# A linear-attention and SwiGLU kernel: other run lengths, orders and queues in the first 65 microseconds

## The chip, the cores and the metric

The kernel runs on one core of a Trainium2 chip. The core has five engines that run side by side, each with its own queue of instructions: PE (TensorE, matrix products and transposes into PSUM), DVE (VectorE), ACT (ScalarE), POOL (GpSimd) and SP (SyncE, which here only issues DMAs). Sixteen DMA engines move data between HBM and the on-chip memory. An engine takes its instructions strictly in the order written; an instruction whose input isn't there holds up all behind it.

The metric is the device time of one execution in microseconds (us), as the median of several. Four runs of the kernel before gave 319.65 us (319.33 to 320.38).

## The reference

Eight batches, eight heads, 576 positions, 64 numbers per head. Per batch and head a state `kv = kᵀ v` (64 by 64) is formed over all 576 positions, and `out = q kv`. Each head's row of `out` is divided by its root mean square and multiplied by `g_norm`. The heads are laid side by side into rows of 512, giving 4608 tokens; these are normalized again by their root mean square and multiplied by `rms_g`, and go through a gated feed-forward layer:

```python
kv = np.einsum('bhsd,bhse->bhde', k, v)
out = np.einsum('bhsd,bhde->bhse', q, kv)
x = (out / rms(out) * g_norm)                  # per head, then heads side by side: 4608 x 512
xn = x / rms(x) * rms_g
g, val = xn @ w_gate, xn @ w_val               # 512 -> 1536, both
y = (g * sigmoid(g) * val) @ w_out             # 1536 -> 512
```

Inputs and output are float32; the kernel computes its products in bf16 and sums in float32.

## The kernel before

The work goes by blocks of 512 tokens. Block n (0 to 7) is the first 512 positions of batch n; the last block, number 8, gathers the 64 positions left over from each batch. For each block the attention part gives `xnt`, the normalized rows turned so that the 512 features lie on partitions (four slices s of 128). The feed-forward part then does, for each of twelve slices j of 128 hidden units, four gate and four value matmuls of 128x512 (`Ffn.up`, L477), a silu on ACT (L482) and a product on DVE (L483); and for each of four row tiles c twelve matmuls with `w_out` (`down_products`, L519) and a copy to `o_sb` and to HBM (`down_out`). The attention of block n+1 is woven into the feed-forward part of block n, so that PE always has matmuls at hand. The order of each engine's instructions is written out by hand; no scheduler moves anything.

The start is different, since nothing is there to weave into. Block 0 is done in two halves of 256 tokens, A and Z (class `Cols`), while the first loads come in. SP's queue has, in this order: k of head pairs 0 and 1 (j = 0, 1; v goes by ACT's queue), half A of the queries (`load_q0(0)`, L585), k and v of pairs 2 and 3, half Z of the queries, the gate weights of blocks 0 and 1 (`load_w`, L178: 256 columns each, all rows), the value weights of blocks 0 and 1 (L182: by halves of the rows, 512 columns), the blocks 2 and 3, block 4 (four slices), then k and v of batch 1, `w_out`, the queries of batches 1 and 2. Each DMA has one of eight semaphores in turn, so a DMA is issued only after the one eight places before it has landed. The staging buffers are seven.

The chain of block 0: k and v are cast to bf16; PE forms the states (`state0`, L254); the queries are cast (`cast_q0`), turned by PE in eight 128x128 transposes per half (`turn_q0`, L642) and copied out of PSUM (`put_q0`, one copy for each two pairs of heads); products of state and turned queries (`columns`, L398) are squared on ACT; PE sums the squares (L419, L422); a short chain of small DVE operations gives the scale per head and row; DVE scales the rows (L458), PE turns them (`x_turn`, L262), DVE copies them to `xnt`. On the way `gam`, holding `rms_g` and `g_norm`, is turned by PE (L712) into columns; their product `rowscale` is multiplied into the rows of the gate and value weights when these are cast to bf16 (`round_w`; L191 on POOL and DVE, L189 on ACT). Wherever PE would idle early, `warm` (L619) puts matmuls of no use.

The first feed-forward matmuls of block 0 (`half_unit`, L494) work on two slices j at a time ("pairs", 0 and 1), for half A while Z is still being prepared: the gates of pair 0 in two parts of 128 tokens, those of pair 1, then the values of pair 0, the two transposes of Z's rows, and the values of pair 1. After that both pairs are done for half Z (in banks named `o_ps` for pair 0), and `Ffn.up` goes on from j = 4 with all 512 tokens, at about 25.8 us.

The load stream that began at 0.7 us keeps the DMA engines busy until about 48 us. Batch 1's queries come in two loads (L135), each of four heads; they are cast and turned by PE (`q_turn`, L833) in the middle of block 0's down products.

At the end of block 0 the queries of batch 2 are cast (`cast_q`, on ACT and DVE) and turned by four DMA transposes on SP's queue (`q_rows`, L300). On SP's queue the four stand between the output DMAs of block 0's first two row tiles and those of the last two, so that they also wait for the first two output copies on ACT. Batch 3's loads (`load_batch`) follow on SP's queue, in step 2 of block 1. PE reads batch 2's turned queries in step 4 of block 1 (L326).

## Time and profile before

| what | value |
|---|---|
| median of four runs | 319.65 us (319.33 to 320.38) |
| profiled execution: its own time | 319.34 us |
| its span, first to last instruction | 317.3 us |
| PE busy | 310.2 us, 98% |
| PE idle before 26 us | 3.24 us |
| mean granted TensorE clock | 0.999 |
| read from HBM, written | 37.75 MB, 9.44 MB |
| DMA issues of half A's queries (L585, two) | 1.63 to 3.06 us |
| PE's first matmuls of half Z's gates into `o_ps` (L494) | 22.29 us |
| the four DMA transposes of batch 2's queries (L300) | issued 56.05 to 63.21 us |

The page gives for each engine its busy time and share of the span. PE is the engine that is always busy after the start; the others have idle time, which costs nothing unless PE waits for them. Where the time between two stretches of PE's work goes is told by the chain of waits: followed back from the last instruction, it names at each step what released it. A line of the chain is: start, length, engine or DMA, tile and line. A line of the windows of busy time is: the window, its length, the busy time of PE, PEld (weight loads), DVE, ACT and POOL with the number of instructions, the granted clock, the DMA share and GB/s. A line of the timeline is: start, busy time, engine, line, operation, tiles and shapes, and in brackets the idle time before it with what ended it; the name in the brackets is inferred and can be another than the true one.

### The profile page before, as it was taken

The page shows a single profiled execution, that of the slowest core. Times are in us where ns is not written, and L with a number is a line of the kernel's source. Part 1 is how long each engine was busy: PE and PEld are TensorE (multiplying, and loading weights), DVE is VectorE, ACT ScalarE, POOL GpSimd, SP SyncE. Part 2 cuts the span into 40 slices and gives each one's busy share as a digit, 9 for nine tenths or more (in the row PEclk, how much of TensorE's full clock was granted, in tenths as well). Part 3 has the DMA queues.
Part 4 walks back from the last instruction along what each step waited for, and adds up shares of the span by engine and source line. Part 5 has one row for each costly group of instructions (what it writes and reads, how often), then busy time and mean ns, then how long its engine had stood idle before and what let it go on. Part 6 is the DMA issues. An engine that isn't in the chain of part 4 may idle for free.

```text
span 317.3 us, 6032 instructions
## 1 busy us (share of the span) xinstructions
PE 310.2 (98%) x2371; PEld 150.4 (47%) x2371; DVE 180.5 (57%) x378; ACT 175.5 (55%) x323; POOL 21.4 (7%) x46
## 2 busy tenths in 40 slices
PE   8899999999999999999999999999999999999995
PEld 3575455444444444444444444444444444444443
DVE  3776668679339913992289327941795079504310
ACT  3577457385667465746683768376845374233321
POOL 1264351100000000000000000000000000000000
PEclk9999999999999999999999999999999999999999
DMA  8999999677479166906790499839003710230014
GB/s 268 364 386 388 375 375 330 136 205 293 106 183 355 54 147 182 366 8 126 186 378 9 108 180 243 301 66 174 29 0 63 145 58 3 60 139 3 0 33 100
DMA packets 60712, 54.95 MB, mean 173 GB/s; under 512 B 36232, under 2 KB 45708, under 8 KB 60684
## 3 DMA queue, kind: packets, MB, share of 16 engines
q1 hardware_dynamic: 60304, 53.92, 57.4%
q10 hardware_dynamic: 380, 0.66, 0.6%
q8 instruction: 18, 0.29, 0.4%
q14 instruction: 10, 0.08, 0.1%
HBM read 37.75 MB, written 9.44 MB: 149 GB/s over the span
## 4 chain that ended last, share of the span: by engine, by line
PE 92%; DMA 5%; SPq 1%; POOL 1%; issue 0%; ACT 0%; DVE 0%
PE g_ps L477 29%; PE v_ps L477 28%; PE o_ps L519 27%; DMA st<-in_moe_w_val_dram 3%; DMA st<-in_q_dram 2%; PE att_ps L286 2%; PE g_ps L519 1%; PE v_ps L519 1%; PE v_ps L494 1%; DMA out_dram<-o_sb 1%; PE att_ps L326 1%; POOL wv_sb L191 1%; PE o_ps L494 1%; PE o_ps L326 0%; PE att_ps L262 0%; SPq L585 0%
## 5 line engine op out<-in xcount | busy, mean ns | idle before, releaser
L483 DVE TENSOR_TENSOR h_sb<-silu,v_ps 128x512 bf16<-128x512 bf16 x104 | 71.1, 683 | 100.2 <-ACT silu L482 68.0
L477 PE MATMUL g_ps<-xnt,wg_sb 128*128 128x512 bf16 x416 | 106.9, 379 | 0.0
L477 PE MATMUL v_ps<-xnt,wv_sb 128*128 128x512 bf16 x416 | 106.8, 379 | 0.0
L482 ACT ACTIVATE silu<-g_ps 128x512 bf16<-128x512 f32 x104 | 62.1, 597 | 70.2 <-PE g_ps L477 54.7
L519 PE MATMUL o_ps<-wo_sb,h_sb 128*128 128x512 bf16 x396 | 87.8, 379 | 0.0
L477 PEld LDWEIGHTS <-wv_sb 128*128 128x128 bf16 x416 | 40.7, 98 | 49.1
L519 PEld LDWEIGHTS <-h_sb 128*128 128x128 bf16 x420 | 40.6, 98 | 47.6 <-issue 0.4
L477 PEld LDWEIGHTS <-wg_sb 128*128 128x128 bf16 x416 | 39.6, 98 | 46.4
L104 ACT COPY o_sb<-o_ps 128x512 f32<-128x512 f32 (+1 forms) x34 | 19.7, 579 | 40.2 <-PE o_ps L519 39.5
L373 DVE TENSOR_TENSOR xna<-outa,s1y 128x512 bf16<-128x512 bf16 x28 | 17.9, 684 | 0.0
L104 ACT CAST vb<-st 128x576 bf16<-128x576 f32 x25 | 15.7, 673 | 3.3 <-DMA st<-in_v_dram 3.3
L104 ACT CAST qb<-st 128x512 bf16<-128x512 f32 (+1 forms) x30 | 16.3, 603 | 2.0 <-DMA st<-in_q_dram 1.9
L356 DVE TENSOR_REDUCE ssq<-sq 128x16 f32<-128x1024 bf16 x14 | 17.1, 1220 | 0.5
L356 DVE TENSOR_REDUCE ssq<-sqt 128x16 f32<-128x1024 bf16 x14 | 17.1, 1220 | 0.5
L104 ACT CAST kb<-st 128x576 bf16<-128x576 f32 x20 | 12.5, 673 | 0.0
L341 ACT ACTIVATE sq<-att_ps 128x512 bf16<-128x512 f32 x14 | 7.6, 594 | 4.3 <-PE att_ps L326 3.6
L619 PE MATMUL att_ps<-kv_all 128*128 128x512 bf16 (+1 forms) x23 | 8.1, 476 | 1.2 <-DVE sel L608 1.2
L355 DVE TENSOR_TENSOR sq<-sq,gsq 128x512 bf16<-128x512 bf16 x14 | 5.9, 422 | 4.9 <-ACT sq L341 4.9
L106 DVE CAST kb<-st 128x576 bf16<-128x576 f32 x12 | 6.0, 517 | 3.6 <-DMA st<-in_k_dram 3.5
L106 POOL CAST wo_sb<-st 128x512 bf16<-128x512 f32 x12 | 7.2, 632 | 7.4 <-DMA st<-in_moe_w_out_dram 7.4
L341 ACT ACTIVATE sqt<-o_ps 128x512 bf16<-128x512 f32 x14 | 7.6, 598 | 0.0
L347 ACT CAST outa<-o_ps 128x512 bf16<-128x512 f32 x14 | 7.5, 592 | 0.0
(148 smaller groups left out, 180.5 us busy)
## 6 DMA issues: line engine op xcount, KB each, us to landing
st<-in_k_dram SPq DMA_DIRECT2D x7, 1152.0 KB, 10.7
st<-in_v_dram SPq DMA_DIRECT2D x7, 1152.0 KB, 12.7
out_dram<-o_sb SPq DMA_DIRECT2D x14, 512.0 KB, 3.1
st<-in_q_dram SPq DMA_DIRECT2D x6, 1024.0 KB, 8.1
st<-in_moe_w_out_dram SPq DMA_DIRECT2D x6, 512.0 KB, 10.4
st<-in_moe_w_gate_dram SPq DMA_DIRECT2D x4, 512.0 KB, 10.3
st<-in_moe_w_val_dram SPq DMA_DIRECT2D x4, 512.0 KB, 9.6
st<-in_k_dram SPq DMA_DIRECT2D x4, 288.0 KB, 4.2
```

What stands on the lines that cost most here:

```text
L104: engine.copy(out=dst, in_=src)
L106: engine.tensor_copy(out=dst, in_=src)
L286: PE.matmul(self.kv_ps[x][to, a, :], lhsT=kb[rows, 2 * a + x, c, :], rhs=vb[rows, 2 * a + x, c, :], start=(a == 0 and c == 0), stop=(a == ...
L341: SC.activation(out=self.in_place(self.sq[i][:, 0], g), in_=bank, func=ACT.Square)
L347: SC.copy(out=self.in_place(rows, g), in_=bank)
L356: DVE.reduce_sum(out=self.ssq[:, c], in_=sq, axis=AX.X)
L373: DVE.tensor_tensor(out=self.xna[c], in0=self.outa[c], in1=self.alpha[:, c, :].to_broadcast([128, H, D]), op=OP.mult)
L477: PE.matmul(ps, lhsT=wt[:, s, j * 128 : (j + 1) * 128], rhs=x[:, s, :], start=(s == 0), stop=(s == NS - 1),)
L482: SC.activation(out=silu, in_=g_ps, func=ACT.Silu)
L483: DVE.tensor_tensor(out=self.h[:, j, :], in0=silu, in1=v_ps, op=OP.mult)
L519: PE.matmul(self.o_ps[c], lhsT=self.h[:, j, c * 128 : (c + 1) * 128], rhs=wo_sb[:, j, :], start=(j == 0), stop=(j == NF - 1),)
L619: PE.matmul(ps[:, 0:w], lhsT=warm_sb[:, 0:128], rhs=warm_sb[:, 0:w], start=True, stop=True, skip_group_check=True)
```

## The change

Five things, all before 65 us:

- Block 0's queries are laid so that a partition holds two heads and eight consecutive positions of each (before: four heads, four positions), in both halves. A contiguous run in HBM is 2 KB instead of 1 KB, a half comes in four DMAs of 32 partitions instead of two of 64. Casts, transposes and copies out of PSUM are as many and as large; a cast takes one head of the two, and a copy out of PSUM takes every fourth element instead of every second. The rows of block 0 so come in another order, and its output is written by four DMAs of 32 partitions for each two row tiles, instead of two of 64.
- The gate weights of blocks 0 and 1 are loaded by halves of the rows, 512 columns wide, as the value weights were; a run is 2 KB instead of 1 KB. POOL's order of rounding follows: rows s = 0, 1 of both blocks, then s = 2, 3 of block 0.
- The value matmuls of pairs 0 and 1 for half A are split by the rows of the weights (s = 0, 1 and s = 2, 3). PE's order is now: pair 0 front, pair 1 front, transpose of Z's first rows, pair 0 back, transpose of the second, pair 1 back. POOL rounds the value weights in the matching order.
- The two small loads of `gam` are issued by POOL, before it makes the identity matrices, instead of by ACT.
- At the end of block 0 all casts and all four transposes of batch 2's queries come first, ahead of all four output copies. On ACT, two casts now precede the copies of the turned rows, and the output copies come after them.

The diff (the parts left out are the loop over `round_w` for the values and the changed slices `hs0`, `hs1`, told above):

```diff
+        def half_units(self, ps, wt, j, lo, ss):
+            for u in range(2):
+                for s in ss:
+                    PE.matmul(
+                        ps[:, u, :], lhsT=wt[:, s, (j + u) * 128 : (j + u + 1) * 128],
+                        rhs=xnts[self.n][:, s, lo : lo + 256],
+                        start=(u == 0 and s == 0), stop=(u == 1 and s == NS - 1), skip_group_check=True,
+                    )
...
-                rows = out[r0 : r0 + 256, :].rearrange("(p c t) d -> t p c d", c=2, t=2)
-                for t in range(2):
-                    nc.sync.dma_start(out=rows[t], in_=self.o_sb[64 * t : 64 * t + 64])
+                rows = out[r0 : r0 + 256, :].rearrange("(p c t) d -> t p c d", c=2, t=4)
+                for t in range(4):
+                    nc.sync.dma_start(out=rows[t], in_=self.o_sb[32 * t : 32 * t + 32])
...
-        dst = q0[:, f].rearrange("(p g) h x -> p g h x", g=2)
-        for g in range(2):
-            src = q[0, 4 * g : 4 * g + 4, 256 * f : 256 * f + 256, :].rearrange("h (p t) d -> p h (t d)", t=4)
+        dst = q0[:, f].rearrange("(p g) h x -> p g h x", g=NS)
+        for g in range(NS):
+            src = q[0, 2 * g : 2 * g + 2, 256 * f : 256 * f + 256, :].rearrange("h (p t) d -> p h (t d)", t=8)
             queue.dma_start(out=dst[:, g], in_=src)
...
-    nc.scalar.dma_start(out=gam[0:NS, :], in_=moe_rms_g.rearrange("(s p) -> s p", p=128))
-    nc.scalar.dma_start(
+    nc.gpsimd.dma_start(out=gam[0:NS, :], in_=moe_rms_g.rearrange("(s p) -> s p", p=128))
+    nc.gpsimd.dma_start(
...
-    load_w("g", (0, 1), False)
-    load_w("v", (0, 1), True)
+    for name in ("g", "v"):
+        load_w(name, (0, 1), True)
...
-        ps = bank.bitcast(BF16).rearrange("p (j t x) -> p j t x", j=2, t=4)
-        for j in range(2):
-            for t in range(4):
-                PE.matmul(
-                    ps[:, j, t, :], lhsT=qb0[:, f, t, 2 * j : 2 * j + 2, :], rhs=identity,
-                    is_transpose=True, start=(j == 0 and t == 0), stop=(j == 1 and t == 3),
-                )
-        return ps.rearrange("p j t (x g) -> p j t x g", g=2)
+        ps = bank.bitcast(BF16).rearrange("p (t x) -> p t x", t=8)
+        for t in range(8):
+            PE.matmul(
+                ps[:, t, :], lhsT=qb0[:, f, t], rhs=identity, is_transpose=True, start=(t == 0), stop=(t == 7),
+            )
+        return ps.rearrange("p t (x g) -> p g t x", g=NS)
...
-    for s in range(NS):
-        round_w(0, "g", s, GP)
-    for s in (0, 1):
-        round_w(1, "g", s, GP)
+    for blk, s in ((0, 0), (0, 1), (1, 0), (1, 1), (0, 2), (0, 3)):
+        round_w(blk, "g", s, GP)
...
-    for u in range(2):
-        ffn.half_unit(first[1], u, wv_sb, u, 0, 256)
-    for u in range(2):
-        x_turn(Z, u, xs[u], DVE)
-    for u in range(2):
-        ffn.half_unit(second[1], u, wv_sb, 2 + u, 0, 256)
+    ffn.half_units(first[1], wv_sb, 0, 0, (0, 1))
+    ffn.half_units(second[1], wv_sb, 2, 0, (0, 1))
+    x_turn(Z, 0, xs[0], DVE)
+    ffn.half_units(first[1], wv_sb, 0, 0, (2, 3))
+    x_turn(Z, 1, xs[1], DVE)
+    ffn.half_units(second[1], wv_sb, 2, 0, (2, 3))
...
-    cast_q(2, 0, SC)
-    ffn.down_out(0)
+    for i in range(T):
+        cast_q(2, i, SC if i < 2 else DVE)
+    atts = {b: Att(b) for b in range(2, B + 1)}
+    for c in range(T):
+        atts[2].q_rows(c)
     down_part(1, 8, 12)
     f_x(0, xs[0], SC)
     f_x(1, xs[1], SC)
-    for i in (1, 2, 3):
-        cast_q(2, i, SC if i == 1 else DVE)
-    ffn.down_out(1)
-    atts = {b: Att(b) for b in range(2, B + 1)}
-    for c in range(2):
-        atts[2].q_rows(c)
     down_part(2, 8, 12)
     f_x(2, xs[2], DVE)
     f_x(3, xs[3], DVE)
     down_part(3, 8, 12)
-    for c in range(2, 4):
-        atts[2].q_rows(c)
-    ffn.down_out(2)
-    ffn.down_out(3)
+    for c in range(T):
+        ffn.down_out(c)
```

## The prediction

> **What bounds the kernel now.** I read the busy shares first, then the windows of busy time, the chain of waits, and the DMA rates by window.
>
> ```profile
> PE 310.2 (98%) x2371; PEld 150.4 (47%) x2371; DVE 180.5 (57%) x378; ACT 175.5 (55%) x323; POOL 21.4 (7%) x46
> 0.00:26.00 26.00, 22.76 (x249) 14.89 (x250) 15.12 (x49) 14.75 (x28) 9.97 (x28) 1.00 0.98 344
> 26.00:311.40 285.40, 285.33 (x2095) 133.65 (x2093) 165.08 (x329) 160.05 (x294) 11.41 (x19) 1.00 0.55 159
> ```
>
> From 26 to 311 us PE idles 0.07 us of 285.4, at full granted clock. The change leaves PE's instruction count alone, so it can only move the moment from which PE runs without a pause (idle before: 3.24 us, plus filler matmuls, L619), or bring a pause in. The chain shows what set that moment, and the one later place where PE paused:
>
> ```profile
> 9.33 8.83 DMA st<-in_moe_w_val_dram
> 18.25 1.85 POOL wv_sb L191 x4
> 20.14 0.83 PE v_ps L494 x6
> 20.97 0.45 PE att_ps L262 x8
> 21.42 0.87 PE v_ps L494 x8
> 22.29 1.75 PE o_ps L494 x16
> 42.60 0.17 PE g_ps L833 x3
> 42.76 0.06 issue
> 42.82 0.44 PE g_ps L833 x5
> ```
>
> The first value weights land at 18.16, four POOL roundings follow, and PE (L494) waits 0.6 us for the fourth. At 42.76 PE waits again, 0.06 us, for batch 1's queries; DVE had waited for their second half to land:
>
> ```profile
> 42.05 0.63 DVE L106 CAST qb<-st 128x512 bf16<-128x512 f32 x2 [0.72 <-DMA st<-in_q_dram]
> 18.25 2.74 POOL L191 TENSOR_SCALAR wv_sb<-st,rowscale 128x256 bf16<-128x256 f32 x6 [1.31 <-DMA st<-in_moe_w_val_dram]
> 14.19 2.74 POOL L191 TENSOR_SCALAR wg_sb<-st,rowscale 128x256 bf16<-128x256 f32 x6 [1.08 <-DVE Az L219]
> ```
>
> So two limits follow one another: PE's start-up order, and the load stream, whose DMA share is about 1 until 48 us. Whatever PE gains early is kept at 42.8 only as far as the stream is early too. The stream's rate depends on what it carries (windows 11 to 14 us, all of it runs of 1 KB, and 18 to 25 us, runs of 2 KB and more):
>
> ```profile
> DMA packets 1057, 1.05 MB, mean 349 GB/s; under 512 B 34, under 2 KB 1057, under 8 KB 1057
> DMA packets 1391, 2.71 MB, mean 387 GB/s; under 512 B 67, under 2 KB 67, under 8 KB 1391
> ```
>
> **Part 1, runs of 2 KB.** Batch 0's queries (1.05 MB) and gate blocks 0 and 1 (1.05 MB) go from 1 KB to 2 KB runs. 2.10 MB takes 6.01 us at 349 GB/s and 5.42 at 387: 0.59 us saved. The first quarter ran beside k and v at some 376 GB/s, where 0.52 MB gains only 0.04 instead of 0.15. Sum: 0.48 to 0.59; I take 0.54. Bounds: 0 (the bytes, not the runs, set the rate) to 0.70 (in the trace a packet of 1 KB took 49.5 ns and one of 2 KB 88; 2048 and 1024 of them over 16 engines are 6.34 and 5.63 us). I take the windows, which count what was moved, overlap of packets included.
>
> The Trainium skill speaks against this ("DMA: Bandwidth & Descriptors", Specifications: transfers reach line rate from 512 B on). By that the term would be 0 and the time 319.6; the two windows differ by 11% with the runs, so the trace decides. No number below uses this rule.
>
> SP issues eight query loads of 128 KB in place of four of 256 KB (1.43 and 1.27 us a pair). A new one has 64 runs; the nearest row is a k issue of 128 runs, 0.33 us, so 8 x 0.33 = 2.6 for 2.7; at the old 0.61 to 0.75 each it would be 5.4. Behind the first four stands a k load that waited for a landing until 4.35 anyway; behind the last four stands the gate load (8.14), which by SP's written order now waits for the eighth DMA before it, a k landing at 8.3. By then over 1 MB is in flight, 3 us of stream, so it costs 0. If that cover failed, each us late is a us lost. Four casts, eight transposes and four copies (0.43 to 0.69 us) keep their counts and sizes; the copies read every fourth element instead of every second. Before, reading every second cost DVE 0.69 for 512 elements, and a plain PSUM copy of 512 elements 0.69 too (45.50): I take 0, at worst 0.6 each.
>
> **Part 2, gate blocks by row halves.** A first half of both blocks lands where block 0 did (14.02, now about 13.55 with 0.47 of the gain by then). POOL rounds it at 2.74/6 = 0.457 each, but block 0's last row piece is now sixth, not fourth: 13.55 + 2.74 = 16.29 instead of 16.02. PE starts that unit at 16.39 (about 0.1 earlier now): cost 0 to 0.3 on PE there, taken as 0.1. Z's sums stand behind on PE; their result has about 0.4 us to spare below.
>
> **Part 3, value pairs by contraction halves.** The transposes for Z stood behind eight value matmuls that needed the fourth rounding. Now, with the landing at 17.62, POOL finishes its six roundings at 18.08, 18.54, 18.99, 19.45, 19.9 and 20.36. PE: first pair's front half 18.8 to 19.2, second's waits for 19.45, ends 19.8; transpose 0 (Z's first scaled rows come by 19.4) to 20.0; first pair's back half 20.4; transpose 1 20.65; second's back half 21.1. The next matmuls (L494, o_ps) start at 21.15 instead of 22.29: 1.1 us earlier. With an unmoved stream it would be 21.8, 0.45 earlier.
>
> **What is kept.** Between 22 and 42 us the stream's consumers have room: value block 4 is rounded by 31.77 for 33.42, and v of batch 1, which landed by 37.7, is cast by 40.80 for 41.28. But batch 1's queries land at 42.05 - 0.54 = 41.5, the casts end at 42.14, and PE, which would be at 41.7, pauses until 42.3. So of the 1.1 us, 0.54 + 0.06 remain at most; I take 0.55.
>
> **Part 4, batch 2's turns in one go.** SP's four transposes move from 56.05 (7.16 us, last landing about 64.4, right when PE wants it at 64.33) to after the casts, about 53.3, ahead of the outputs; they queue behind batch 2's k and v, so those are not delayed. Without this the earlier PE would wait here for up to 0.55 us; with it there are some 3 us of room. The outputs become eight issues of 128 KB behind the turns. On ACT the second query cast (0.63) now precedes the copies of rows, and four output copies go last: the last one ends about 0.15 later, before PE needs its bank at 57.38. PE cost 0. Batch 3's loads stand behind eight issues on SP, 0.33 to 0.6 each, instead of four: start 63.5 to 65.5 against 64.60, used after 75: 0.
>
> **Part 5, norm weights from POOL.** Both loads of the norm weights go from ACT, which then waited for v until 4.53, to POOL, ahead of the identity matrix. POOL was idle 10.92 us until 12.50, and PE wants the identity at 8.09 and the weights (L712) at 10.16. No row shows a DMA issued by POOL; ACT's two took 0.55 and 0.69. With those the weights are under way by 2 us: cost 0, nothing to gain. The upper end: the slowest issue in these rows, 4.35 us, twice, from 0.7 on, and 3.6 us to land as the first k did: 13.0, 2.8 us late. I take 0, since rows of the same two loads are nearest. "DMA: Bandwidth & Descriptors" (Anatomy of one DMA) puts a fixed 2.0 us on each DMA that POOL issues; by it they land near 5 us, and the trace of before has none to show it.
>
> **Sum.** The profiled execution took 319.34 (span 317.3); 319.34 - 0.55 = 318.8. The median of the four runs is 0.31 above the profiled one: 319.1.
>
> **Rivals.** (a) PE's whole 1.1 us is kept, since the queries land still earlier than the rate says. For it: in the trace fifteen of the sixteen DMA engines had brought the first value half by 16.84, and the last one, which seems to have served a 16 KB instruction fetch (1.12 us at 15.40), at 18.16; such a lag can be smaller. Time 319.65 - 1.1 = 318.5. (b) Longer runs do not speed the stream; then the queries still land at 42.05 and only 0.06 is left: 319.6. Against it stand the windows. (c) Slower: the norm weights issued by POOL land late, and PE's in-order queue stops at L712 with batch 0's columns behind it. PE can lose 0.55 there free, until 10.7 (it would wait at 42 anyway), and the next 0.55 eats the saving; from 11.3 us on the time is above that of before, us for us, and landing at 13.0 gives 319.65 + 1.7 = 321.4. For it: no such row exists; against it: 8 us of room. (d) The lag of the slowest DMA engine grows by another instruction fetch before the queries: 1.12 more on them, less 0.54: 319.65 + 0.55 = 320.2. For it: the trace has two such fetches by 26 us, and the runs spread over 1.05 us; against it: the fetches follow PE's instruction count, which is unchanged.
>
> **How the numbers follow.** A change under 0.3% (0.96 us) can hardly be told from none. Forecast 0.46 (318.7 to 319.4), (a) 0.24, (b) 0.13, (c) 0.08, (d) 0.09. (a), with the upper end of part 1, is faster by over 0.3% (0.24), and a fifth of the forecast's cases (0.09): 0.33. Slower: (c), 0.04 of (d) (a further fetch), and 0.04 for copies that double: 0.16. Same: the rest, 0.51. Range 318.1 (all of PE's gain and a little) to 320.3 ((d)); this leaves (c) and the far end of (a) out.
>
> **What would show it.** The DMA rate over 11 to 14 us near 385 GB/s; POOL's first value rounding near 17.6; L494 into o_ps near 21.2; a longer pause than 0.06 at the query turns near 42; the turns on SP near 53.5. I am wrong if the norm weights hold PE up at L712, if PE idles between 16 and 19, or if the queries of batch 1 land as late as before.

## The result, and the profile after

The changed kernel takes 320.3 us (median of 51 runs, 319.68 to 324.33) against 319.81 us for the kernel before on the same chip (76 runs, 318.76 to 321.01). The ratio is 1.0023, 95% interval 1.0015 to 1.0031; like the ratios below, it is not the quotient of the two medians (here 1.0015). I had forecast 319.1 us. The kernel became slightly slower, by less than 0.3% but clear of its interval, and the forecast had the wrong sign.

The windows of busy time of the kernel after (start and end in us; length; busy time and instructions of PE, PEld, DVE, ACT and POOL; granted clock; DMA share; GB/s):

```profile
0.00:26.00 26.00, 20.38 (x235) 13.41 (x236) 14.79 (x48) 13.80 (x25) 10.39 (x27) 1.00 0.93 330
26.00:312.80 286.80, 286.79 (x2110) 134.97 (x2108) 165.28 (x330) 161.14 (x296) 12.38 (x21) 1.00 0.55 160
10.50:12.00 1.50, 1.42 (x31) 0.85 (x32) 1.34 (x5) 0.95 (x3) 0.00 (x0) 1.00 0.87 305
12.00:13.50 1.50, 1.35 (x30) 0.80 (x28) 0.69 (x5) 0.89 (x4) 0.61 (x1) 1.00 0.86 283
13.50:15.00 1.50, 1.50 (x21) 1.24 (x22) 0.89 (x5) 0.65 (x2) 0.00 (x0) 1.00 0.90 276
```

From 26 us on PE idles 0.01 us, so the whole loss lies in the first 26. There the stream of loads is thin: 276 to 305 GB/s with DMA engines idle (share 0.86 to 0.90, where the full stream below has 1.06 to 1.09) in just the stretch in which I expected 385; over 11 to 14 us it is 281. The same windows of the kernel before have full engines:

```profile
10.50:12.00 1.50, 1.35 (x23) 0.67 (x21) 1.22 (x7) 0.87 (x2) 0.00 (x0) 1.00 1.08 333
12.00:13.50 1.50, 1.36 (x22) 0.99 (x22) 0.62 (x5) 0.89 (x2) 0.61 (x1) 1.00 1.06 355
13.50:15.00 1.50, 1.45 (x15) 0.82 (x13) 1.05 (x5) 0.66 (x2) 0.81 (x2) 1.00 1.09 363
```

SP's queue tells why (timeline of SP: start, us, line, DMA, count). The kernel after:

```profile
1.64 2.71 SPq L595 DMA_DIRECT2D st<-in_q_dram  x4
...
6.77 2.54 SPq L595 DMA_DIRECT2D st<-in_q_dram  x4
9.35 1.10 SPq L182 DMA_DIRECT2D st<-in_moe_w_gate_dram  x2
```

The kernel before:

```profile
1.63 1.43 SPq L585 DMA_DIRECT2D st<-in_q_dram  x2
...
6.82 1.27 SPq L585 DMA_DIRECT2D st<-in_q_dram  x2
8.14 1.15 SPq L178 DMA_DIRECT2D st<-in_moe_w_gate_dram  x2
```

A query load costs SP 0.64 to 0.72 us on average, whether it is 256 KB or 128 KB. Eight of them take 5.25 us instead of 2.70, and the gate loads go out at 9.35 instead of 8.14. The chain of waits of the kernel after carries this on to PE:

```profile
9.98 7.76 DMA st<-in_moe_w_gate_dram
17.74 0.08 issue
17.82 1.10 POOL wg_sb L191 x2
...
18.97 0.45 PE g_ps L494 x5
...
23.71 1.91 PE o_ps L494 x16
...
44.18 0.45 PE g_ps L841 x8
```

The second gate half, issued at 9.98, lands at 17.74; POOL rounds it, and PE, which could have gone on at 17.2, waits. Part of this landing is the lag of one DMA engine: by the landing records of the sixteen engines, fifteen had brought their shares by 16.45 and the last at 17.74, 1.29 us later. Without part 1 (the first experiment below) the sixteen bring this half within 14.23 to 15.13. So the late issue and the thin stream account for about 1.3 us of the landing (16.45 against 15.13), and the one engine for the rest. The waits of PE over the first 30 us have the line

```profile
PE g_ps L494 <- POOL wg_sb L191: 1.6, 2, 1.3
```

that is, 1.6 us in two waits, the longest 1.3. The matmuls of L494 into o_ps start at 23.71, against 22.29 before and 21.15 forecast. Those 1.42 us, less the 0.06 that PE no longer pauses at batch 1's query turns (44.18), are the 1.32 us between the two profiled executions (320.66 and 319.34). Over all runs the medians differ by 0.5: the profiled execution of the kernel before was 0.47 below its median and that of the kernel after 0.36 above. How thin the stream gets and how the engines finish differ from trace to trace: a later kernel with the same loads (the one with more fillers) had 202, 318 and 332 GB/s in the same three windows, and its second gate half landed at 16.55, the last engine 0.06 us behind the fifteenth.

### The profile page after: what moved, and what is told of

It is laid out like the page before. It is cut to its first block, busy times and chain, and to the rows that moved or that the text cites. A ratio compares the mean times of both kernels' runs of the same rounds, so it can differ in the third digit from the quotient of the medians.

```text
span 318.8 us, 6049 instructions
## 1 busy us (share of the span) xinstructions
PE 309.1 (97%) x2371; PEld 150.1 (47%) x2371; DVE 180.4 (57%) x378; ACT 175.6 (55%) x323; POOL 22.8 (7%) x48
## 4 chain that ended last, share of the span: by engine, by line
PE 92%; DMA 5%; SPq 1%; POOL 0%; DVE 0%; issue 0%; ACT 0%
PE g_ps L477 29%; PE v_ps L477 28%; PE o_ps L529 27%; DMA st<-in_moe_w_gate_dram 2%; DMA st<-in_q_dram 2%; PE att_ps L286 2%; PE g_ps L494 1%; PE g_ps L529 1%; PE v_ps L529 1%; SPq L595 1%; DMA out_dram<-o_sb 1%; PE att_ps L326 1%; PE o_ps L494 1%; PE o_ps L326 0%; PE att_ps L262 0%; PE v_ps L503 0%
## 5 line engine op out<-in xcount | busy, mean ns | idle before, releaser
L347 ACT CAST outa<-att_ps 128x512 bf16<-128x512 f32 x14 | 7.5, 593 | 0.0
```

Source lines behind the costliest of these rows:

```text
L347: SC.copy(out=self.in_place(rows, g), in_=bank)
```

## The experiments

All times are medians with those of the kernel before on the same chip, and the ratio with its 95% interval. The parts are numbered as in the prediction. Theory Q is the one formed from the profile after: the gate loads are issued late, because of the number of loads ahead of them.

**The change without part 1** (queries as before; everything else as after).

```diff
-        for g in range(NS):
-            src = q[0, 2 * g : 2 * g + 2, 256 * f : 256 * f + 256, :].rearrange("h (p t) d -> p h (t d)", t=8)
+        for g in range(2):
+            src = q[0, 4 * g : 4 * g + 4, 256 * f : 256 * f + 256, :].rearrange("h (p t) d -> p h (t d)", t=4)
             queue.dma_start(out=dst[:, g], in_=src)
...
```

> The changed kernel with part 1 undone: block 0's queries in 1 KB runs, two loads of 64 partitions per half. Theory Q (the eight query loads, each as long on SP's queue as one of the old four, are what thins the load stream: 276 to 305 GB/s between 10.5 and 15 us where the kernel before had 333 to 363): the stream is back above 340 GB/s there, the second gate half lands near 15.3 instead of 17.7, PE's wait at the first gate unit (1.3 us) shrinks below 0.3, and the time is 0.5 to 1.0 us under the kernel before, near 319.0. Theory G (the gate blocks' row halves run slowly by themselves): the stream stays near 280 to 300 GB/s while they are moved and the time stays near 320.4. Theory P (the norm weights on POOL's queue disturb the stream): also unchanged.

Measured: 318.97 us against 319.71, ratio 0.9978 (0.9967 to 0.9989). Its timeline of SP and its windows:

```profile
5.76 1.27 SPq L595 DMA_DIRECT2D st<-in_q_dram  x2
7.08 1.18 SPq L182 DMA_DIRECT2D st<-in_moe_w_gate_dram  x2
```

```profile
10.50:12.00 1.50, 1.50 (x32) 0.84 (x25) 1.28 (x7) 0.95 (x3) 0.00 (x0) 1.00 1.07 372
13.50:15.00 1.50, 1.50 (x17) 0.92 (x15) 1.01 (x6) 0.58 (x3) 1.05 (x3) 1.00 1.06 392
```

The gates go out 2.3 us earlier than after, the stream is whole, L494 into o_ps starts at 21.49, batch 1's queries land at 41.43, and PE waits for no gate rounding. In the profiled pair the gain is 319.34 - 318.80 = 0.54 us, but 318.80 is the fastest of its ten executions. I ran it a second time beside later kernels.

> The kernel after without part 1 once more, beside the next two, so that they can be compared on one chip and so that its 0.9978 is seen a second time. Theory Q: 0.997 to 0.9985, full clock in nearly all runs. If it comes out at 1.000 or above, the earlier gain was the chip's.

Measured: 319.02 against 319.87, 0.998 (0.9966 to 0.9994). By the medians the gain is 0.74 and 0.85 us. So parts 2 to 5 gain what I had forecast for the whole, and part 1 costs about 1.3 us. The profiled execution of this second run, 319.43, was the slowest of its twelve: o_ps started at 21.87, the value halves landed at 16.85 and 19.07 and batch 1's queries at 42.05, against 17.55, 18.91 and 41.43 in the first. Landings and starts of a single execution can thus differ by up to 0.7 us for one and the same kernel.

**The change without part 2** (gates by blocks of columns, as before).

```diff
-    for name in ("g", "v"):
-        load_w(name, (0, 1), True)
+    load_w("g", (0, 1), False)
+    load_w("v", (0, 1), True)
...
```

> The changed kernel with part 2 undone: gate blocks 0 and 1 as two loads of 256 columns in 1 KB runs, POOL's rounding order with them. Theory Q: the stream still dips to about 300 GB/s before 13 us, PE waits about 0.5 to 1 us for the first gate block, time 320 to 320.5. Theory G: no dip, the first gate block lands near 14, no wait of PE before 19 us, time 319.0 to 319.4. Theory P: the dip stays.

Measured: 320.65 against 319.71, 1.0041 (1.0025 to 1.0057). The late gates are the same (9.28), the stream falls to 253 and 240 GB/s in 10.5 to 13.5 us, and PE now waits 0.7 us for value roundings. Part 2 is not what hurts.

**The change without part 5** (norm weights on ACT).

```diff
-    nc.gpsimd.dma_start(out=gam[0:NS, :], in_=moe_rms_g.rearrange("(s p) -> s p", p=128))
-    nc.gpsimd.dma_start(
+    nc.scalar.dma_start(out=gam[0:NS, :], in_=moe_rms_g.rearrange("(s p) -> s p", p=128))
+    nc.scalar.dma_start(
```

> The changed kernel with part 5 undone: both loads of the norm weights issued by ACT again. Theory P: the stream is back above 350 GB/s between 10.5 and 15 us and the time under 319.3. Theories Q and G: nothing changes beyond 0.2 us, 320.2 to 320.6, with the same dip.

Measured: 321.56 against 319.71, 1.0073 (1.0046 to 1.01), where I had expected nothing. SP's timeline:

```profile
1.63 3.97 SPq L595 DMA_DIRECT2D st<-in_q_dram  x4
...
10.30 1.10 SPq L182 DMA_DIRECT2D st<-in_moe_w_gate_dram  x2
```

The first four query loads take 3.97 us instead of 2.71: a load is issued only when the one eight issues before it on SP and ACT together has landed, and the two norm weight loads take two of these eight turns. The third and fourth query loads go out at 4.36 and 5.01, the third 0.01 us after the first k landed (4.35). Everything behind is late by about 1 us more, and the stream from 6 to 9 us is at 285 GB/s. The execution with the profile was the fastest of ten; in seven of the ten the mean granted clock was 0.987 to 0.995, which is part of the loss.

**Parts 3 and 4 alone, on the kernel before** (value pairs by contraction halves; batch 2's turns in one go).

```diff
-    for blk, s in ((0, 0), (0, 1), (1, 0), (0, 2), (1, 1), (1, 2)):
+    for blk, s in ((0, 0), (0, 1), (1, 0), (1, 1), (0, 2), (1, 2)):
         round_w(blk, "v", s, GP)
...
```

> The kernel before with parts 3 and 4 alone: value pairs by halves of the rows, batch 2's turns first; all loads as before. By the prediction's steps: PE starts the second half's gates about 0.45 us earlier (21.8 instead of 22.3), the queries of batch 1 still land at 42.0, so only 0.06 us is kept: 319.7, within 0.1 of the kernel before. If the order itself costs, the time is above by 0.3 or more.

Measured: 319.45 against 319.71, 0.9993 (0.9981 to 1.0005). L494 into o_ps starts at 21.69, 0.6 earlier than before; the waits of PE then have

```profile
PE g_ps L843 <- DVE qb L106: 0.6, 1, 0.6
```

The gain is given back in full at batch 1's query turns, whose loads land at 42.34, as "What is kept" said. Its loads are those of the kernel before, and yet the stream had 278 GB/s in 10.5 to 12 us in this trace, where that kernel had 333: a thin window is not peculiar to late gates.

**Number of loads or length of runs.** Without part 1, but each of the four query loads split in two by heads: eight loads of 128 KB in runs of 1 KB.

```diff
-            queue.dma_start(out=dst[:, g], in_=src)
+            for hs in (slice(0, 2), slice(2, 4)):
+                queue.dma_start(out=dst[:, g, hs], in_=src[:, hs])
```

> The kernel after without part 1 (queries in runs of 1 KB, four heads on 64 partitions), but each of the four query loads of 256 KB split by heads into two of 128 KB: the number and the size of the loads are those of the kernel after, the length of the runs and the number of partitions are not. Theory Q (the number of loads is the cause: SP needs about 0.6 us for each, whatever its size, and eight small loads leave too few bytes in flight): SP's second four to eight query issues take 2.4 to 2.6 us, the gate loads go out at 9.2 to 9.5 us instead of 7.1, the stream falls to 280 to 340 GB/s in 6 to 9 us and to about 300 in 10.5 to 15, the second gate half lands after 17 us, PE waits over 1 us for its rounding; time 1.001 to 1.004 of the kernel before. Rival R (runs of 2 KB onto every fourth partition are what thins the stream): the stream holds 365 to 390 GB/s from 10.5 us on, PE waits for no gate rounding, time 0.997 to 0.999 as without part 1.

Measured: 320.96 against 319.3, 1.0051 (1.0033 to 1.0069). SP's timeline and the windows:

```profile
6.56 2.56 SPq L596 DMA_DIRECT2D st<-in_q_dram  x4
9.17 1.11 SPq L182 DMA_DIRECT2D st<-in_moe_w_gate_dram  x2
```

```profile
12.00:13.50 1.50, 1.22 (x24) 0.77 (x20) 0.58 (x5) 0.78 (x4) 0.61 (x1) 0.72 0.99 303
13.50:15.00 1.50, 1.50 (x16) 1.14 (x14) 0.91 (x5) 0.62 (x2) 0.07 (x1) 0.50 0.89 320
```

The number alone brings back the late gates, a thin stream (share 0.99 and 0.89) and the loss; rival R falls. The detail of the forecast did not hold: the second gate half landed at 16.11, not after 17, and PE did not wait for its rounding. L494 into o_ps started at 22.92; PE had waited 1.2 us for v of pair 2 and ran at half the granted clock from about 12.7 to 16 us. The clock is not the whole loss, since three executions with a mean granted clock of 0.999 took 320.79 to 321.40 us; where those lost their time no trace shows.

**Parts 2, 3 and 4** (parts 1 and 5 undone, by the two edits shown for them).

> The kernel after without parts 1 and 5: queries and norm weights as before, gates by row halves, value pairs by contraction halves, batch 2's turns in one go. Theory Q: with four query loads of 256 KB over 1 MB is in flight whatever queue the norm weights take, so part 5 alone is worth 0 to 0.2 us and this kernel stands at 0.9975 to 0.9985, as the one without part 1 did (0.9978). Rival N (moving the norm weights off ACT is itself what gains, as its undoing cost 1.6 us in the profiled pair of the kernel after): this kernel stands at 1.000 or above, with v's first loads or the query loads of SP issued later and a stream below 340 GB/s in 6 to 9 us.

Measured: 319.33 against 319.3, 1.0007 (0.9986 to 1.0027). Rival N was right in its number, as far as so wide an interval tells, and not in its window (392 GB/s in 6 to 9 us). With the norm weights on ACT the gates go out at 8.45, not 7.08: the third k load waits again for its turn, from the first k's landing (issued at 4.39, landed at 4.38), where it went out at 3.12 without them. Then 10.5 to 12 us is at 322 GB/s. Part 5, which I had put at 0, is worth 0.3 us by the medians of the two kernels and 0.9 by their ratios, whose intervals overlap.

**Half Z's queries issued by POOL** (the kernel after, with that one edit).

```diff
-    load_q0(1, nc.sync)
+    load_q0(1, nc.gpsimd)
```

> The kernel after, but the four query loads of the second 256 rows are issued by POOL behind the norm weights instead of by SP. Theory Q: SP no longer spends 2.54 us on them and they take none of the eight places in turn, so the gate loads go out at about 6.8 to 7.4 us instead of 9.35 and 9.98, over 1 MB is in flight, the stream is above 360 GB/s from 10.5 us on, the second gate half lands before 15.5, PE waits at most 0.3 us for the gate rounding, o_ps of L494 starts at 21.2 to 21.8; time 0.997 to 0.999. Rival P (loads issued by POOL land late or hold POOL up: four of about 0.6 us put the identity matrix at 5.8 us, and if they take as long as the norm weights to land, about 5 us, or 2 us more for each in a row, the second half's columns are late): PE waits for qb or att_ps of the second half before 12 us, time 1.000 to 1.004.

Measured: 320.08 against 319.3, 1.0039 (1.0008 to 1.007). Theory Q's half holds: gate loads at 6.94, the stream at 375 to 397 GB/s in every window from 6 us on, gates at 13.63 and 14.99, although the queries still come in eight small loads in runs of 2 KB. But POOL, which waits for none of the eight turns, issued them by 4.73 us, ahead of k and v of pairs 2 and 3, and these landed up to 1 us later (12.27 for the last). The waits of PE and two windows:

```profile
PE att_ps L651 <- DVE kv_all L669: 1.9, 1, 1.9
```

```profile
10.50:12.00 1.50, 0.75 (x20) 0.58 (x18) 0.79 (x2) 1.16 (x2) 0.00 (x0) 0.89 1.04 390
12.00:13.50 1.50, 1.50 (x12) 0.62 (x10) 1.04 (x6) 0.58 (x2) 0.00 (x0) 0.50 1.04 397
```

So the time was lost at another place than rival P named. L651 is the turn of half A's queries, which are still issued by SP: beside POOL's loads the fourth of them landed at 8.74, against 7.47 in the kernel after, and the last casts of half A's queries ran at 8.84 on ACT and 8.86 on DVE, against 7.57 and 7.59. The wait line names the state `kv_all`, but its copy (DVE, 9.20) stands behind that cast in DVE's order. Half A's queries and k and v of pairs 2 and 3 came late, not half Z's queries. The profiled execution, at 321.64, was also well above the median, with a mean granted clock of 0.993.

**2 KB runs in two loads a half.** The kernel after, one load of 256 KB for each head of the four pairs, on all 128 partitions.

```diff
-        for g in range(NS):
-            src = q[0, 2 * g : 2 * g + 2, 256 * f : 256 * f + 256, :].rearrange("h (p t) d -> p h (t d)", t=8)
-            queue.dma_start(out=dst[:, g], in_=src)
+        src = q[0, :, 256 * f : 256 * f + 256, :].rearrange("(g h) (p t) d -> h g p (t d)", g=NS, t=8)
+        for h in range(2):
+            queue.dma_start(out=q0[:, f, h], in_=src[h])
...
-        return ps.rearrange("p t (x g) -> p g t x", g=NS)
+        return ps.rearrange("p t (g x) -> p g t x", g=NS)
```

> The kernel after, but each half of batch 0's queries in two loads of 256 KB instead of four of 128 KB: all 128 partitions in one load, one head on a partition and load, runs of 2 KB kept; the partition is group times 32 plus row group, and the copies after the transposes read 32 neighbours instead of every fourth element. Theory Q: with the number of loads back at four, SP's issues take about 1.3 us a pair, the gate loads go out at about 7.1 us, no thin stretch from 6 to 15 us (above 360 GB/s in each), PE waits at most 0.3 us for gate roundings, o_ps of L494 starts at 21.2 to 21.6; time 0.9965 to 0.9985. Part 1's own term (2 KB runs speed the stream by 0.5 us for 2.1 MB, of which the gates' share is already in the kernel without part 1): 0.2 to 0.3 us less than that kernel, value halves landing 0.2 to 0.3 earlier than 17.55 and 18.91. Rival R (runs of 2 KB themselves thin the stream): 280 to 310 GB/s in 10.5 to 15 us again, time 1.001 to 1.004.

Measured: 331.29 against 319.87, 1.037 (1.0346 to 1.0393), far from every theory. Its windows and waits of PE:

```profile
9.00:10.50 1.50, 0.00 (x0) 0.00 (x0) 0.00 (x0) 0.00 (x0) 0.00 (x0) 1.00 1.05 206
12.00:13.50 1.50, 0.00 (x0) 0.00 (x0) 0.00 (x0) 0.00 (x0) 0.00 (x0) 0.50 0.26 97
```

```profile
PE att_ps L650 <- ACT qb L104: 6.5, 1, 6.5
PE att_ps L650 <- POOL qb L106: 4.3, 1, 4.3
```

The records of the single DMA engines show the cause: twelve of the sixteen had brought their share of the third k by 7.83 us, the other four by 14.32 to 14.78, since these four alone brought the query loads. The outermost dimension of these loads is the four pairs. The Trainium skill has the rule ("DMA: Bandwidth & Descriptors", "Why a DMA increments its semaphore by 16 and not by 1"): the number of engines is the largest up to 16 that divides the slowest dimension of both sides. Four engines for a dimension of four is what this run shows. The same load with the 32 row groups outermost:

```diff
+        src = q[0, :, 256 * f : 256 * f + 256, :].rearrange("(g h) (p t) d -> h p g (t d)", g=NS, t=8)
+        for h in range(2):
+            queue.dma_start(out=q0[:, f, h], in_=src[h])
```

> As the kernel after, each half of batch 0's queries in two loads of 256 KB with runs of 2 KB, but now with the 32 row groups as the outermost dimension of the load and the four head pairs inside (the form before, with the four pairs outermost, was brought in by four of the sixteen engines). The partition is row group times 4 plus pair, as in the kernel after, so copies and transposes are those of the kernel after. Theory Q with the outermost dimension as what spreads a load: all sixteen engines bring each query load, SP's issues take about 1.3 us a pair, the gate loads go out near 7.1 us, 360 GB/s or more in each window from 6 to 15 us, PE waits at most 0.3 us for gate roundings; time 0.9965 to 0.9985. Part 1's own term (2 KB runs speed the stream): value halves land 0.2 to 0.3 us earlier than without part 1 (17.55 and 18.91) and the time is 0.2 to 0.3 us below 319.0; if the bytes alone set the rate, they land within 0.1 of it. Rival R (2 KB runs thin the stream whatever the count): 280 to 310 GB/s in 10.5 to 15 us, 1.001 to 1.004.

Measured: 319.2 against 319.61, 0.9984 (0.9973 to 0.9995). The windows:

```profile
10.50:12.00 1.50, 1.50 (x41) 0.93 (x38) 1.46 (x6) 0.95 (x3) 0.00 (x0) 1.00 1.05 399
13.50:15.00 1.50, 1.50 (x21) 1.15 (x19) 1.02 (x5) 0.58 (x3) 0.94 (x3) 1.00 1.05 388
```

With four loads the 2 KB runs do no harm: rival R falls again, and all engines bring each load. They also bring nothing: the value halves land at 17.66 and 18.93 and batch 1's queries at 41.45, against 17.55, 18.91 and 41.43 with queries in 1 KB runs.

**Fillers where PE waits** (the kernel after; four more filler matmuls in the first gate unit, ahead of the third row piece).

```diff
+                if (lo, u, s) == (0, 0, 2):
+                    warm(second[0].rearrange("p u t -> p (u t)"), 4)
```

> The kernel after with four more filler matmuls of 512 columns (0.9 to 1.5 us) on PE in the first gate unit, where PE waits 1.3 us for the rounding of the second gate half. Theory C (an idle stretch of PE of more than a microsecond lowers the granted clock for some microseconds, and this is part of what the kernel after loses: a quarter of its runs have a mean clock below 0.998, and are up to 4 us longer): nearly all runs at 0.998 or above, none above 321 us, median unchanged within 0.2 us, mean 0.2 to 0.4 us lower. Rival W (the lowered clock comes from somewhere else, or by chance): as many lowered runs as in the kernel after, one in four, and the same spread. Either way the loads land as in the kernel after and o_ps of L494 starts at 23.5 to 23.9.

Measured: 320.2 against 319.87, 1.0019 (1.0005 to 1.0032). One of 12 executions had a mean granted clock of 0.995 or less, against 9 of 52 of the kernel after (the profiled one included) and 8 of 125 of the kernel before; none was above 321.04. That is too few to tell C from W. L494 into o_ps started at 23.08 in the profiled execution, earlier than I had said. The median is that of the kernel after, so the clock is not its main loss.

**Part 5 alone, on the kernel before** (its two lines as in the diff of the change).

> The kernel before with part 5 alone: the two norm weight loads issued by POOL instead of ACT. Theory Q (a load's turn comes when the one eight loads before it has landed, and the two norm weights took two of the eight turns): the gate loads go out at 7.1 to 7.5 us instead of 8.14 and 8.78, the first value half lands near 17.6 instead of 18.16, batch 1's queries near 41.4 instead of 42.05, o_ps of L494 starts about 0.5 earlier than 22.29 with the old order of PE, and PE does not wait at batch 1's query turns; time 0.998 to 0.9995 of the kernel before. Rival T (the gain needs parts 2, 3 and 4 as well, since PE's start order, not the stream, sets when it runs without a pause): the stream is early, but o_ps of L494 starts within 0.2 of 22.29; time 0.9995 to 1.001. My prediction's own value for part 5 alone was 0.

Measured: 319.32 against 319.69, 0.999 (0.9978 to 1.0001). The windows and the chain:

```profile
12.00:13.50 1.50, 1.35 (x21) 0.84 (x19) 0.58 (x4) 0.87 (x3) 0.61 (x1) 1.00 1.10 349
13.50:15.00 1.50, 1.50 (x19) 1.03 (x17) 1.01 (x6) 0.58 (x3) 0.78 (x2) 1.00 1.09 363
```

```profile
8.79 9.39 DMA st<-in_moe_w_val_dram
...
22.32 1.75 PE o_ps L494 x16
```

The gates go out at 7.12, as Theory Q said, but the first value half lands at 18.19 and o_ps starts at 22.32, as before; rival T had o_ps right, though not its early stream. The median is 0.37 us lower, with an interval that reaches just past 1. Early issue alone hardly helps, since the engines are already full (1.09) at 349 to 363 GB/s, with the gates in runs of 1 KB. The next kernel adds part 2, and with it the gates' runs of 2 KB.

**Parts 2 and 5, on the kernel before.**

```diff
+    nc.gpsimd.dma_start(out=gam[0:NS, :], in_=moe_rms_g.rearrange("(s p) -> s p", p=128))
...
-    load_w("g", (0, 1), False)
-    load_w("v", (0, 1), True)
+    for name in ("g", "v"):
+        load_w(name, (0, 1), True)
...
+    for blk, s in ((0, 0), (0, 1), (1, 0), (1, 1), (0, 2), (0, 3)):
+        round_w(blk, "g", s, GP)
```

> The kernel before with parts 2 and 5 alone: gate loads by row halves in runs of 2 KB, norm weights issued by POOL; queries, value order and turns as before. If the gates' longer runs are what moves the stream (part 5 alone left the first value half at 18.19 us, with gates of 1 KB runs at 349 to 363 GB/s): the gates land by 13.8 and 15.1, the first value half near 17.6, batch 1's queries near 41.45 instead of 42.05, and o_ps of L494 starts near 21.75 (0.55 earlier, with PE's old order); no wait at batch 1's query turns but perhaps one at batch 2's, as PE runs 0.5 us early there and the turns stand where they did; time 0.998 to 0.9995. If part 3 is needed for the gain: 0.9995 to 1.0005, with o_ps within 0.2 of 22.29.

Measured: 319.05 against 319.72, ratio 0.9991 (0.9977 to 1.0006; two of the twelve executions, at a mean clock of 0.993 and 0.995, were above 320). The windows and the chain:

```profile
12.00:13.50 1.50, 1.30 (x18) 0.84 (x20) 0.63 (x4) 0.84 (x3) 0.61 (x1) 1.00 1.03 382
13.50:15.00 1.50, 1.50 (x18) 0.98 (x16) 1.01 (x6) 0.58 (x3) 1.02 (x3) 1.00 1.06 392
```

```profile
21.64 1.75 PE o_ps L494 x16
```

Against part 5 alone the gates' runs of 2 KB bring the first value half from 18.19 to 17.48 and batch 1's queries from 42.05 to 41.37. In the profile this holds nearly the whole gain of the kernel without part 1, whose o_ps starts at 21.49; its interval reaches 1.0006, so by the times alone it isn't told from the kernel before. The 0.7 us rest on single executions, and the second profile of the kernel without part 1, with the same gate runs, had 16.85 for the first value half and 42.05 for the queries: only the rate is seen in every trace. In the two windows from 12 to 15 us the six traces with gate runs of 2 KB and a full stream have 382 to 397 GB/s, and the three with 1 KB have 349 to 366. Over these 3 us that is about 0.24 us (an estimate from the two pairs of windows of these kernels: 31 of 387 GB/s), not 0.7.

**Late gates with large query loads.** The kernel without part 1, with four tiny loads ahead of the gates; they bring 4 KB each into a tile that nothing reads.

```diff
     load_q0(1, nc.sync)
+    junk = consts.tile([32, 4, 2, 16], FP32, name="junk")
+    for i in range(4):
+        nc.sync.dma_start(out=junk[:, i], in_=q[0, 2 * i : 2 * i + 2, 0:32, 0:16].rearrange("h p d -> p h d"))
```

> The kernel without part 1 (0.9978 and 0.998), with four tiny extra loads on SP just ahead of the gate loads: each brings 4 KB of queries (64 pieces of 64 bytes) into a tile that nothing reads. The query loads keep their 256 KB. Theory Q (what costs is that the gate loads are issued late: about 0.6 us of SP and one of eight turns for every load ahead of them, whatever its size): SP spends 1.8 to 2.5 us on the four, the gate loads go out at 9.0 to 9.7 us, some window between 10.5 and 15 us falls below 330 GB/s, the second gate half lands at 16 to 18 us, PE waits for its rounding or for the columns ahead of it; time 1.001 to 1.004. Rival S (the small size of the query loads, 128 KB, thins the stream, by what is under way at once): the gate loads may go out late, but the stream holds 365 GB/s or more, the second gate half lands by 15.7, time 0.998 to 0.9995.

Measured: 320.53 against 319.72, 1.0026 (1.001 to 1.0043). SP's timeline and two windows:

```profile
7.10 2.51 SPq L613 DMA_DIRECT2D junk<-in_q_dram  x4
10.02 1.15 SPq L182 DMA_DIRECT2D st<-in_moe_w_gate_dram  x2
```

```profile
10.50:12.00 1.50, 1.50 (x24) 0.73 (x24) 1.25 (x6) 0.87 (x2) 0.00 (x0) 1.00 1.00 262
13.50:15.00 1.50, 1.41 (x14) 0.78 (x12) 1.05 (x5) 0.70 (x3) 0.95 (x3) 1.00 0.96 298
```

With sixteen KB of extra data in four loads the stream has 262 and 298 GB/s in these windows, and the kernel takes 1.5 us more than the same kernel without them. The turns are seen one by one: the third and fourth tiny loads go out at 8.48 and 9.29, and the gate loads at 10.02 and 10.78, each 0.01 to 0.02 us after the load eight places before had landed (8.46, 9.28, 10.00, 10.76). Rival S falls. But the second gate half landed at 15.40, earlier than I had said, although it was issued at 10.78, later than in the kernel after (9.98, landed at 17.74). So the time of issue alone doesn't set the landing. In the profiled execution (319.83, the second fastest of ten) o_ps starts at 22.05, 0.6 us later than without the tiny loads; the rest of its loss there comes at batch 1's query turns, whose second half lands at 42.21 instead of 41.43.

## Why the prediction was wrong, step by step

**The step that failed** is in part 1: "By then over 1 MB is in flight, 3 us of stream, so it costs 0". SP's issues took 5.25 us, not 2.6; I had priced a 128 KB query load by its 64 runs from the k loads' row (0.33), and named 5.4 as the other bound. By that bound the gates had to go out about 1.3 us later, and I let 1 MB in flight cover it. The cover did not hold: the engines idled for 10 to 14% of 10.5 to 15 us, the second gate half landed at 17.74, and o_ps started 2.56 us after the forecast. The sentence behind it, "each us late is a us lost", fits this profile only in its total: 1.21 us late at SP and 1.42 us late on PE against the kernel before, whose order of work is another; against the kernel without part 1, with the same order, 2.27 and 2.22. Of the landing at 17.74, 1.29 us is the lag of one DMA engine, which my sum did not have, and the tiny loads' gates went out 1.88 us later than before with o_ps 0.24 us earlier. That the number of loads ahead does it, and not the length of their runs or their size, is shown by the eight loads of 1 KB runs (1.0051), the four loads of 2 KB runs (0.9984) and the tiny loads (1.0026).

**Part 1's gain** of 0.54 us did not come from the queries: their longer runs bring none that can be seen (four loads of 2 KB runs). The gates' longer runs, which come with part 2's edit, raise the rate; the 0.7 us at the value weights and at batch 1's queries (parts 2 and 5 against part 5 alone) rests on one execution of each, and the rate explains about 0.24 of it. The rule of the Trainium skill that I set aside ("DMA: Bandwidth & Descriptors", Specifications: line rate from 512 B on) fits the queries and not the gates: 349 and 363 GB/s at 1 KB, 382 and 392 at 2 KB, in the same windows. The copies after the transposes cost nothing more, 0.68 and 0.58 us, as taken.

**Part 2** held: with the gates on time PE waits for none of their roundings. **Part 3** held in kind: o_ps at 21.49 without part 1 and at 21.69 on the unmoved stream, where I had 21.15 and 21.8. **"What is kept"** held in kind: the gain of parts 3 and 4 alone ends in a 0.6 us wait at batch 1's query turns. That parts 2 to 5 gain 0.54 us in the first profiled pair, where I had kept 0.55, is luck: the second profiled execution of that kernel was 0.09 us slower than that of the kernel before, and the medians gain 0.74 and 0.85. **Part 4** held: the turns start at 55.37 in the kernel after, 2 us later than forecast (PE itself is 2.6 us later than forecast), and land by 61.83 against 64.4 before; batch 3's loads start at 67.03, later than my 65.5, and nothing waits for them.

**Part 5** failed in its price, too. The norm weights did land early (6.55 us), so rival (c) did not come. But "cost 0, nothing to gain" overlooked what the description of the kernel before says: each load takes one of eight turns, and two loads off ACT free two of them. The gates then go out at 7.08 instead of 8.45, and without it parts 2, 3 and 4 show no gain (1.0007, with an interval of 0.9986 to 1.0027, against 0.9978 and 0.998).

**The rivals.** (d) gave nearly the measured time, 320.2, by a DMA engine lagging behind an instruction fetch. One engine did lag, by 1.29 us, at the second gate half and not at the queries that (d) named; the fetch of 16 KB started at 17.41, when the other fifteen had long been done (16.45), so it isn't shown that the fetch made this lag. In other traces a lag of this size does follow the fetch: without part 1 the fetch started at 15.37, and the first value half was there from fifteen engines at 16.46 and from the last at 17.55. The main loss stands without the lag: fewer loads ahead of the gates undo it, and more bring it back. What came, late gate loads, I had named as a condition and not as a rival. (a) and (b) did not come.

**What stays open.** Why engines idle while bytes are waiting: at 11 us the kernel after has issued 1.8 MB that have not moved, the one without part 1 2.7 MB, and only the first is thin. The runs show the dependence on the number of loads ahead of the gates; by the tiny loads the time of issue alone doesn't set the landing, and what happens between issue and first byte isn't seen. Nor is it known how often one engine lags as it did in the profile. How much of the late issue is SP's own time and how much the eight turns differs by kernel: after, the fourth load's issue ended at 9.31 and the turn was free at 9.07, so SP's time decided; with the tiny loads the turns did.

## What to carry to other kernels

Count a queue's loads, not only its bytes: before halving the size of a load, look up what one issue costs and which earlier load has to land before it may go, and follow both to the first load behind that someone waits for. Two small loads moved off a shared set of turns let the weights go out 1.0 to 1.4 us earlier here; by themselves neither they (0.999, up to 1.0001) nor the reordering of the work (0.9993, up to 1.0005) are clear of their intervals, while together, with the gates in runs of 2 KB, they are. When runs are made longer, do it where the number of loads stays the same, as in the weights here, and look how many DMA engines bring the load: with 32 row groups outermost all sixteen did, with four pairs outermost only four. The kernel without part 1, 0.9978 and 0.998 of the kernel before, beats both kernels.

## What the hardware showed that I had not expected

- The issue of a query load on SP takes 0.55 to 0.77 us at 128 KB and at 256 KB alike, and 0.31 to 0.62 us for 4 KB in 64 pieces.
- A load whose outermost dimension is four is brought by four of the sixteen DMA engines; the k and v loads behind them landed only at 14.78 to 17.06 (1.037).
- PE's granted clock fell to 0.50 from about 11.7 to 15 us after PE had waited 1.9 us, around 7.6 to 9.5, with half Z's queries on POOL, and from 12.7 to 16 with eight loads of 1 KB runs, where PE idled 1.2 us from 9.2. The Trainium skill ("TensorE: Matmul & The Clock Gate", "HAM oscillation — how this bites in real kernels") sets the limit at idle gaps of about 3.4 us; these are shorter. Gaps of nearly the same length left the clock alone: PE idled 1.24 us from 9.27 in the kernel with the gates as before, and 1.3 us in the kernel after. So what sets the limit isn't settled here.
